# Attention in another written order: projections grouped, six leading key units, weight clamps on GpSimd

## The chip, the cores and the metric

The kernel runs on one core of one Trainium2 chip. The metric is the device time of one execution in microseconds (us), the median of several runs.

## What is computed

```python
def phi(x):
    proj = np.einsum('bhsd,df->bhsf', x, w_phi)
    proj = proj - np.max(np.abs(proj), axis=-1, keepdims=True)
    return np.concatenate([np.exp(proj), np.exp(-proj)], axis=-1)
q_p, k_p = (phi(q), phi(k))
kv = np.einsum('bhsf,bhsd->bhfd', k_p, v)
z = np.sum(k_p, axis=2)
num = np.einsum('bhsf,bhfd->bhsd', q_p, kv)
den = np.einsum('bhsf,bhf->bhs', q_p, z)[..., None] + 1e-06
attn_out = num / den          # 8 batches, 8 heads, 576 tokens, 64 wide; 128 features

x = attn_out, heads side by side          # 4608 x 512
h = x @ w_in                              # 512 x 2048
g = h * np.tanh(softplus(h))
out = g @ w_out                           # 2048 x 512
```

## The kernel before, in words

The program has two stages. The first, some 272 us, is the attention; the second is the feed-forward network, which forms its products from split weights (a rounded part and the rest, each product taken three times) and reads the attention's output back from device memory. Beside the attention, 16 pieces of the feed-forward weights are converted: a piece is loaded as 64-bit words, and GpSimd, VectorE and ScalarE make 32-bit values of them.

The order of every engine's work is written by hand. Each operation is registered with a time, `at(time, function, ...)`; at the end all are sorted by that time and issued in that order. The times set nothing but the order: each engine, and each DMA queue (all transfers here are issued by SP), works through its own instructions in the order written and waits for what it needs.

The attention has 36 units of keys and 36 units of queries (`NU`), each of 512 rows of a pair of heads. The keys run ahead of the queries by `LEAD` units; then a step takes one unit of each.

- A key unit: `k_load` (SP), `k_proj` (TensorE, 16 matmuls into a buffer of the pool `ps_a`, which has two for keys and queries together), `k_center` (VectorE: the largest absolute value, L270, and the subtraction, L271), `k_exp` (ScalarE: two exponentials, L315 and L316), `k_sum` (TensorE, L318, tile names kvps: e times v, accumulated over the rows of a pair of heads). A pair of heads has 4.5 tiles of 128 rows, so every ninth tile is shared by two pairs; a unit with a shared tile has 80 matmuls of sums instead of 64. When a pair's rows are all in, `k_store` (ScalarE, L341) copies its sums out of PSUM. `v_load` (SP) fetches a pair's values into one of three buffers.
- A query unit: `q_load`, `q_proj` (TensorE, pp_q), `q_center` (VectorE), `q_turn` (TensorE, dt: 16 transposes of the centred projection into two PSUM banks), `q_exp` (ScalarE, L371, four exponentials, two for each bank), `q_num` (TensorE, num: the exponentials times the pairs' sums, into two PSUM banks), `q_den` (ScalarE, L391), `q_norm` (VectorE: the reciprocal, L396, and the division, L399), `q_out` (TensorE, xt: four transposes of x), `q_store` (ScalarE, L415, and a DMA to device memory).
- dt, num, xt and the sums share the pool `ps_b` of four PSUM banks.
- TensorE's tile shapes: projections and dt have 64 rows and 128 columns, xt 128 by 128, sums and num 128 rows and 64 columns, the shared tile's sums 64 rows.
- A weight piece: an absolute value on ScalarE (L164), clamp, shift, sign and scale on VectorE (L167, L171, L175, L181), then `low` on GpSimd (L185 and L187), and either a total, four sums, a cast on ScalarE (L215) and a difference, or the cast and two more on GpSimd. The shift reads what the clamp wrote.

The order of one step on TensorE is: quotients of unit n, sums, dt of the next unit, keys' projection, x's transposes, queries' projection. The steps' times are `base(step)` plus constants: `L_AT` for the leading key units, `K_AT` and `Q_AT` for the steps, `T_AT` for the last query units. Weight pieces are due every 14.719 (`CONV`), that is two steps:

```python
at(t + a[0], k_proj, u)
at(t + a[1], k_center, u)
at(t + a[2], k_exp, u)
at(after + a[3], k_sum, u)
at(after + a[4], k_store, u)
...
at(end + a[4], q_num, u)
at(end + a[5], q_den, u)
at(end + a[5] + 0.05, q_norm, u)
at(close_by + a[6], q_out, u)
```

Of the kernel before, what the change touches and what calls it, by code (L numbers as in the profile page):

```python
# [16 lines left out]
P = 128  # L17
# [31 lines left out]
CONV = (13.41, 14.719)  # L49
# [26 lines left out]
def attention_then_mish(ctx, tc, qT, kT, va, w_phi, w_in, w_out, w_out2, out):  # L76
# [71 lines left out]
    def weight_ops(kind, fp, k, quiet):  # L148
# [17 lines left out]
        def clamp():  # L166
            nc.vector.tensor_scalar(w(), w(), LARGE, SMALL, op0=ALU.min, op1=ALU.max)  # L167
# [10 lines left out]
        def scale():  # L178
            t = mid.tile([P, 512], F32, tag="t", name=f"t_{kind}_{fp}_{k}", bufs=1)
            piece[key].append(t)  # L180
# [36 lines left out]
        def lo():  # L217
            dst = piece[key][3]
# [3 lines left out]
        def rest():  # L222
            dst = piece[key][3]
            eng.tensor_sub(w(), w(), dst[:, 0].bitcast(F32))

        def lo_out():
            dst = piece[key][3]
# [3 lines left out]
        def done():  # L231
            staged[key] = piece.pop(key)[3]
# [3 lines left out]
        def spill(h):  # L236
            dst = piece[key][3] if key in piece else staged[key]
# [6 lines left out]
        rest_ops = [(2.2, low)]  # L244
# [20 lines left out]
    def center(parts, name):  # L265
        e = att.tile([P, 2, 2, 512], F32, tag="e", name=f"e_{name}", bufs=5)
        m = att.tile([P, 2, 4], F32, tag="m", name=f"m_{name}", bufs=4)
        to = e[:, :, 0, :].rearrange("p j (n f) -> p j n f", f=F)
        for a, b, ps in parts:
            nc.vector.tensor_reduce(m[:, :, a:b], ps[:, :, a:b], axis=AX.X, op=ALU.max, apply_absolute_value=True)  # L270
# [11 lines left out]
    kv, kv_ps, v_live, k_live = {}, {}, {}, {}  # L282
# [24 lines left out]

    def k_center(n):
        k_live[n] = center(k_live.pop(n), f"k_{n}")

    def k_exp(n):
        e = k_live[n]
        for a, b in zip(cuts_of(n), cuts_of(n)[1:]):
            cols = slice(a * P, b * P)
            nc.scalar.activation(e[:, :, 1, cols], e[:, :, 0, cols], AF.Exp)  # L315
            nc.scalar.activation(e[:, :, 0, cols], e[:, :, 0, cols], AF.Exp, scale=-1.0)  # L316

    def k_sum(n):  # L318
        es = k_live.pop(n)
        tiles = [list(pairs_of(t)) for t in range(4 * n, 4 * n + 4)]  # L320
        for i in sorted(range(4), key=lambda i: len(tiles[i])):
# [6 lines left out]
            for j in range(2):  # L328
                for s in range(2):
                    for r, (p, slot) in enumerate(tiles[i]):  # L330
                        rows = slice(r * D, (r + 1) * D) if shared else slice(0, P)
                        halves(kv_ps[p][:, j, s], es[rows, j, s, i * P:(i + 1) * P], (v_live[p][rows, slot, j, :],) * 2,
                               start=(p in fresh and j == s == 0), stop=(slot == 4))
            for p, slot in tiles[i]:
                if slot == 4:
                    del v_live[p]

    def k_store(n):
# [626 lines left out]
```

## Time and profile before

| | |
|---|---|
| median of 3 runs | 1021.35 us (1021.35, 1023.08, 1020.93) |
| span of the profiled execution | 1021.3 us; its own time beside the span is not given apart from the three runs |
| TensorE busy | 1008.5 us (99%) |
| VectorE, ScalarE, GpSimd busy | 733.3 (72%), 497.7 (49%), 307.1 (30%) us |

In the rows below PE is TensorE's matmuls, PEld its weight loads, DVE VectorE, ACT ScalarE, POOL GpSimd, SP the queue that issues the transfers. L262 is line 262 of the kernel. A timeline's row has the start and the length in us, the engine, the line, the operation, out<-in, the count, and in brackets the idle time before it with what ended it. A matmul's end is modelled; the distance of starts is what two neighbours cost. A row that groups instructions has busy us and the mean of one in ns, then the idle time before them.

### The profile page before, as it was taken

The page shows a single profiled execution, that of the slowest core. Times are in us where ns is not written, and L with a number is a line of the kernel's source. Part 1 is how long each engine was busy: PE and PEld are TensorE (multiplying, and loading weights), DVE is VectorE, ACT ScalarE, POOL GpSimd, SP SyncE. Part 2 cuts the span into 40 slices and gives each one's busy share as a digit, 9 for nine tenths or more (in the row PEclk, how much of TensorE's full clock was granted, in tenths as well). Part 3 has the DMA queues.
Part 4 walks back from the last instruction along what each step waited for, and adds up shares of the span by engine and source line. Part 5 has one row for each costly group of instructions (what it writes and reads, how often), then busy time and mean ns, then how long its engine had stood idle before and what let it go on. Part 6 is the DMA issues. An engine that isn't in the chain of part 4 may idle for free.

```text
span 1021.3 us, 28170 instructions
## 1 busy us (share of the span) xinstructions
PE 1008.5 (99%) x12136; PEld 952.4 (93%) x12136; DVE 733.3 (72%) x1161; ACT 497.7 (49%) x863; POOL 307.1 (30%) x263
## 2 busy tenths in 40 slices
PE   8999999999999999999999999999999999999998
PEld 7889999998889999999999999999999999999998
DVE  6999999988568867658576572466767667667666
ACT  5778777877665434344343433343332333333322
POOL 0454435544513464544746430001101001011011
PEclk9999999999999999999999999999999999999999
DMA  6555567776698676476655768983362451532621
GB/s 208 184 179 184 176 209 256 250 240 200 250 337 311 256 263 219 153 261 243 213 208 172 262 216 313 367 320 105 124 227 65 164 189 60 207 140 88 228 83 42
DMA packets 89292, 208.62 MB, mean 204 GB/s; under 512 B 7376, under 2 KB 35792, under 8 KB 86352
## 3 DMA queue, kind: packets, MB, share of 16 engines
q1 hardware_dynamic: 89168, 206.83, 57.8%
q8 instruction: 95, 1.56, 0.6%
q14 instruction: 29, 0.24, 0.1%
HBM read 122.91 MB, written 83.89 MB: 202 GB/s over the span
## 4 chain that ended last, share of the span: by engine, by line
PE 97%; ACT 1%; DVE 1%; issue 1%; DMA 0%; SPq 0%; DVEq 0%; ACTq 0%
PE h L486 35%; PE o L613 19%; PE o L636 18%; PE num L279 7%; PE kvps L279 7%; PE pp_q L262 4%; PE pp_k L262 3%; PE dt L366 2%; PE xt L408 2%; ACT e_q L371 0%; DMA kraw<-kT 0%; ACT xc L454 0%; DVE m_q L270 0%; DVE x L399 0%; PE z L636 0%
## 5 line engine op out<-in xcount | busy, mean ns | idle before, releaser
L486 PE MATMUL h<-xc,win 128*128 128x256 f32 x3024 | 381.5, 283 | 0.3 <-DVE u L514 0.3
L486 PEld LDWEIGHTS h<-xc,win 128*128 128x128 f32 x3024 | 375.3, 192 | 6.1 <-DVE u L514 0.5
L613 PE MATMUL o<-wout,gh 128*128 128x512 f32 x576 | 144.3, 392 | 0.0
L708 POOL TENSOR_TENSOR part<-part,du 128x512 f32<-128x512 f32 x18 | 23.4, 1298 | 387.9 <-DVE du L698 387.9
L613 PEld LDWEIGHTS o<-wout,gh 128*128 128x128 f32 x576 | 103.6, 189 | 18.7
L518 DVE TENSOR_TENSOR u<-h,u 128x512 f32<-128x512 f32 x72 | 49.6, 688 | 95.2 <-PE h L486 95.1
L636 PE MATMUL o<-wa,gh 128*128 128x256 f32 x576 | 104.4, 282 | 0.0
L636 PEld LDWEIGHTS o<-wa,gh 128*128 128x128 f32 x576 | 88.6, 190 | 0.1
L636 PE MATMUL o<-wa,gl 128*128 128x256 f32 x288 | 80.2, 283 | 0.0
L279 PE MATMUL kvps<-v,e_k 128*64 128x65 f32 (+1 forms) x2560 | 77.2, 222 | 1.6 <-issue 1.6
L636 PE MATMUL o<-wb,held 128*128 128x256 f32 x636 | 77.9, 282 | 0.2 <-DVE du L698 0.2
L636 PEld LDWEIGHTS o<-wb,held 128*128 128x128 f32 x636 | 76.9, 188 | 0.4 <-DVE du L698 0.4
L613 PE MATMUL o<-wout,gl 128*128 128x512 f32 x288 | 77.1, 389 | 0.0
L279 PE MATMUL num<-kv,e_q 128*64 128x65 f32 x2304 | 76.5, 223 | 0.6 <-ACT e_q L371 0.4
L371 ACT ACTIVATE e_q<-dt 128x512 f32<-128x512 f32 x144 | 74.4, 604 | 4.7 <-PE dt L366 4.2
L279 PEld LDWEIGHTS num<-kv,e_q 128*64 128x64 f32 x2304 | 71.2, 137 | 5.4 <-ACT e_q L371 1.2
L279 PEld LDWEIGHTS kvps<-v,e_k 128*64 128x64 f32 (+1 forms) x2560 | 72.5, 137 | 3.7 <-issue 2.1
L506 DVE TENSOR_TENSOR u<-h,p 128x256 f32<-128x256 f32 x72 | 30.1, 418 | 56.2 <-ACT p L493 56.2
L534 ACT ACTIVATE sb<-h 128x256 f32<-128x256 f32 x36 | 13.8, 384 | 105.1 <-PE h L486 71.2
L613 PEld LDWEIGHTS o<-wout,gl 128*128 128x128 f32 x288 | 54.0, 188 | 11.5 <-DVE gl L555 0.4
L493 ACT COPY p<-h 128x256 f32<-128x256 f32 x72 | 26.4, 366 | 69.5 <-PE h L486 69.1
L537 ACT ACTIVATE u<-u 128x768 f32<-128x768 f32 x36 | 30.5, 846 | 56.6 <-DVE u L518 56.6
(99 smaller groups left out, 1662.5 us busy)
## 6 DMA issues: line engine op xcount, KB each, us to landing
xc_spill<-xc SPq DMA_DIRECT2D x63, 512.0 KB, 4.1
xc<-xc_spill SPq DMA_DIRECT2D x63, 512.0 KB, 5.1
x<-x_spill SPq DMA_DIRECT2D x22, 512.0 KB, 6.4
o_part<-part SPq DMA_DIRECT2D x11, 1024.0 KB, 5.0
part<-o_part SPq DMA_DIRECT2D x11, 1024.0 KB, 5.9
in_spill<-wst_in SPq DMA_DIRECT2D x24, 448.0 KB, 2.7
win<-in_spill SPq DMA_DIRECT2D x12, 896.0 KB, 6.8
v<-va SPq DMA_DIRECT2D x32, 325.0 KB, 3.9
```

The costliest lines, as they stand in the source:

```text
L262: nc.tensor.matmul(ps[:, j, n], src, w_phi2[rows], start=True, stop=True)
L279: nc.tensor.matmul(ps[rows], lhsT[:, rows], rhs[h], start=start, stop=stop, skip_group_check=True)
L366: nc.tensor.transpose(turned[n, h][:, jj, i], e[rows, jj, 0, i * P:(i + 1) * P], ident[rows, rows])
L371: nc.scalar.activation(e[:, s, h], ps, AF.Exp, scale=2.0 * s - 1.0)
L486: nc.tensor.matmul(ps, w, x, start=(i in (0, 2) and m == 0), stop=(m == 5), skip_group_check=True)
L493: nc.scalar.copy(p1, h_live[n][0][:, 0])
L506: nc.vector.tensor_tensor(u2, hx[:, 1], u_live[n][0], op=ALU.add)
L518: nc.vector.tensor_tensor(u[:, 0:3:2] if second(n) else u[:, 1:3], hy, u2.unsqueeze(1).broadcast_to([P, 2, CH]), op=ALU.add)
L537: nc.scalar.activation(u[:, 0:3], u[:, 0:3], AF.Mish)
L613: nc.tensor.matmul(o_live[s][tt], g[:, 2 * f + which, cols], wout[fp][:, f, k], start=(first and g is gh and f == k == 0), stop=(last and ...
L636: nc.tensor.matmul(ps, g, w, start=(start and k == 0), stop=(stop and k == 2), skip_group_check=True)
L708: nc.gpsimd.tensor_tensor(cross, cross, d_live[s, tau][0].unsqueeze(1).broadcast_to([P, 2, CH]), op=ALU.add)
```

## The change

The steps' order on TensorE becomes: queries' transposes, queries' projection, keys' projection, the sums of a shared tile, x's transposes of an earlier unit, sums of one or two tiles, quotients, sums of the last two tiles. Six key units lead instead of four. The quotients are formed bank by bank, and each bank gets its own division (a reciprocal each). The largest value and the subtraction of a key unit become two operations of VectorE's order, with the first half of a query unit's division between them; the two exponentials of a key unit are apart in the same way on ScalarE. A pair's sums are stored as soon as all its tiles are in, at either of two places of a step. The weight clamps of the first 16 pieces go to GpSimd, `low` is cut in two (`low`, `scaled`), and a piece's operations get times of their own within four steps.

```diff
--- before.py
+++ after.py
-LEAD = 4
-LEAD_STEP = 3.04
-L_AT = (0.0, 2.62, 3.19, 7.71, 9.38)
-STEP = 7.341
+LEAD = 6
+LEAD_STEP = 3.0
+ENDING = 4
+STEP = 6.95
 TAIL_STEP = 5.73
-LOAD_AT = (-10.994, -0.87, -9.498, -12.558)
-V_AT = (-5.9, -5.9, -5.9, 4.4, 2.0)
+LOAD_AT = (-8.7, 0.3, -10.5, -12.558)
+V_AT = (-5.9, -5.9, -5.9, -2.0, -2.0)
-K_AT = (-1.011, 1.881, 3.585, 3.13, 4.2)
-Q_AT = (1.52, 3.149, 6.11, 6.455, 1.875, 3.0, 6.564, 9.042)
+K_AT = (1.37, 3.9, 5.7, 3.85, 5.0, 2.3, 2.87, 3.1, 5.68, 6.3)
+Q_AT = (0.48, 1.45, 0.0, 0.7, 1.9, 3.81, 4.9, 5.1, 6.1, 0.01, 2.41, 3.2)
 T_AT = (0.95, 2.19, 4.9, 5.3, 8.55, 10.92, 12.6, 13.1)
+BITS_AT = (6.4, 7.0, 14.2, 14.25, 21.15)
+SUMS_AT = (7.1, 21.6, 22.9, 24.2, 24.8, 25.4, 26.0, 27.2, 28.2)
+PLAIN_AT = (7.1, 21.6, 20.3, 23.0, 24.4)
-CONV = (13.41, 14.719)
...
         def clamp():
-            nc.vector.tensor_scalar(w(), w(), LARGE, SMALL, op0=ALU.min, op1=ALU.max)
+            (nc.vector if quiet else nc.gpsimd).tensor_scalar(w(), w(), LARGE, SMALL, op0=ALU.min, op1=ALU.max)
...
             nc.gpsimd.tensor_scalar(f, piece[key][0][:, 0], 2.0 ** -52, None, op0=ALU.mult)
+
+        def scaled():
+            f = piece[key][1][:, 4:8].rearrange("p b m -> p (b m)")
             t = piece[key][2]
             nc.gpsimd.tensor_tensor(t, f, t, op=ALU.mult)
...
-    def center(parts, name):
+    def largest(parts, name):
+        m = att.tile([P, 2, 4], F32, tag="m", name=f"m_{name}", bufs=4)
+        for a, b, ps in parts:
+            nc.vector.tensor_reduce(m[:, :, a:b], ps[:, :, a:b], axis=AX.X, op=ALU.max, apply_absolute_value=True)
+        return parts, m
+
+    def center(parts, m, name):
...
-    def k_exp(n):
+    def k_exp(n, signs=(1, 0)):
         e = k_live[n]
         for a, b in zip(cuts_of(n), cuts_of(n)[1:]):
             cols = slice(a * P, b * P)
-            nc.scalar.activation(e[:, :, 1, cols], e[:, :, 0, cols], AF.Exp)
-            nc.scalar.activation(e[:, :, 0, cols], e[:, :, 0, cols], AF.Exp, scale=-1.0)
+            for s in signs:
+                nc.scalar.activation(e[:, :, s, cols], e[:, :, 0, cols], AF.Exp, scale=2.0 * s - 1.0)
+
+    def k_order(n):
-    def k_sum(n):
-        es = k_live.pop(n)
         tiles = [list(pairs_of(t)) for t in range(4 * n, 4 * n + 4)]
-        for i in sorted(range(4), key=lambda i: len(tiles[i])):
+        order = sorted(range(4), key=lambda i: -len(tiles[i]))
+        shared = [i for i in order if len(tiles[i]) == 2]
+        rest = order[len(shared):]
+        return shared, rest[:2 - len(shared)], rest[2 - len(shared):]
+
+    def k_sum(n, part):
...
+        for i in k_order(n)[part]:
...
-    def k_store(n):
-        for p in [p for p in sorted(kv_ps) if (p + 1) * S <= (n + 1) * 512]:
+    def k_store():
+        for p in [p for p in sorted(kv_ps) if left[p] == 0]:
...
-        for j in range(2):
-            for i in range(2):
+        for i in range(2):
+            for j in range(2):
                 for t in range(2):
...
+    def q_norm(n, i):
+        x, r = x_live[n], r_live[n]
+        nc.vector.reciprocal(r[:, i], r[:, i])
+        nc.vector.tensor_tensor(x[:, i].rearrange("p t (j d) -> p t j d", d=D), num_live.pop((n, i))[:, :, :, :D],
+                                r[:, i].unsqueeze(3).broadcast_to([P, 2, 2, D]), op=ALU.mult)
...
-        return min(step, NU - LEAD) * STEP + max(0, step - NU + LEAD) * TAIL_STEP
+        return min(step, NU - ENDING) * STEP + max(0, step - NU + ENDING) * TAIL_STEP
...
+        t, at_exp, at_sum = base(u - LEAD), base(u - LEAD + 1), base(u - LEAD + 2)
+        a = K_AT
         if u < LEAD:
...
+            at(t - 11.1, k_load, u)
+            at(t + V_AT[min(u, 4)], v_load, u)
+            at(t, k_proj, u)
+            at(t + 0.5, k_first, u)
+            at(t + 1.0, k_exp, u)
+        else:
+            at(t + LOAD_AT[0], k_load, u)
+            at(t + LOAD_AT[1], v_load, u)
+            at(t + a[0], k_proj, u)
+            at(t + a[1], k_largest, u)
+            at(t + a[2], k_center, u)
+            at(at_exp + a[3], k_exp, u, (1,))
+            at(at_exp + a[4], k_exp, u, (0,))
+        if u < LEAD - 2:
+            at(at_sum + (-0.1 if u == 0 else 1.2), k_sum, u, 0)
+            at(at_sum + (-0.1 if u == 0 else 1.2), k_sum, u, 1)
+            at(at_sum + 1.3, k_sum, u, 2)
+            at(at_sum + 2.0, k_store)
+        else:
+            at(at_sum + a[5], k_sum, u, 0)
+            at(at_sum + a[6], k_sum, u, 1)
+            at(at_sum + a[7], k_store)
+            at(at_sum + a[8], k_sum, u, 2)
+            at(at_sum + a[9], k_store)
...
+        at(t + a[0], q_proj, u)
+        at(t + a[1], q_center, u)
+        at(after + a[2], q_turn, u)
+        at(after + a[3], q_exp, u, 0)
+        at(after + a[4], q_exp, u, 1)
+        at(after + a[5], q_num, u)
+        at(after + a[6], q_den, u, 0)
+        at(after + a[7], q_norm, u, 0)
+        at(after + a[8], q_den, u, 1)
+        at(max(end + a[9], after + a[8] + 0.1), q_norm, u, 1)
+        at(end + a[10], q_out, u)
+        at(end + a[11], q_store, u)
...
+        if i < 4 * HALF:
+            t = base(2 * i)
+            at(t - 8.0, weight_load, *pc)
+            for delay, (_, op) in zip(BITS_AT, bits):
+                at(t + delay, op)
+            times = SUMS_AT if len(sums) == len(SUMS_AT) else PLAIN_AT
```

## Rows read from the trace of the kernel before

**Rows 1.** The page: busy us, share of the span, instructions.
```profile
PE 1008.5 (99%) x12136; PEld 952.4 (93%) x12136; DVE 733.3 (72%) x1161; ACT 497.7 (49%) x863; POOL 307.1 (30%) x263
```

**Rows 2.** The chain of waits, first 300 us, shares by line.
```profile
by line: PE num L279 23.7%; PE kvps L279 22.4%; PE pp_q L262 12.0%; PE pp_k L262 11.5%; PE dt L366 6.6%; PE xt L408 6.2%; PE h L486 5.2%; PE o L613 2.9%; issue 2.1%; ACT e_q L371 1.6%; DMA kraw<-kT 1.4%; ACT xc L454 0.9%; DVE m_q L270 0.8%;
```

**Rows 3.** Stages, us: PE, PEld, DVE, ACT, POOL busy, clock, DMA, GB/s.
```profile
176.96:184.27 7.31, 7.31 (x199) 6.76 (x200) 6.92 (x9) 5.39 (x11) 5.99 (x7) 1.00 0.61 218
...
sum 36.11, PE 36.11 PEld 33.57 DVE 34.10 ACT 28.34 POOL 21.75; mean PE 7.22 PEld 6.71 DVE 6.82 ACT 5.67 POOL 4.35
```

**Rows 4.** Timeline of PE, one step without a shared tile.
```profile
184.20 2.11 PE L279 MATMUL num<-kv,e_q 128*64 128x65 f32 x64
186.12 2.06 PE L279 MATMUL kvps<-v,e_k 128*64 128x65 f32 x64
188.11 0.71 PE L366 MATMUL dt<-ident,e_q 64*128 64x64 f32 x16
188.66 1.11 PE L262 MATMUL pp_k<-head,kraw 64*128 64x128 f32 x16
189.70 0.66 PE L408 MATMUL xt<-ident,x 128*128 128x128 f32 x4
190.28 1.16 PE L262 MATMUL pp_q<-head,qraw 64*128 64x128 f32 x16
191.37 2.08 PE L279 MATMUL num<-kv,e_q 128*64 128x65 f32 x64
```

**Rows 5.** Timeline of PE, a query projection right behind a key projection.
```profile
22.22 1.16 PE L262 MATMUL pp_k<-head,kraw 64*128 64x128 f32 x16
23.22 1.06 PE L262 MATMUL pp_q<-head,qraw 64*128 64x128 f32 x16
```

**Rows 6.** Timeline of PE, xt followed by a matmul of its shape.
```profile
279.68 0.60 PE L408 MATMUL xt<-ident,x 128*128 128x128 f32 x4
280.03 3.84 PE L486 MATMUL h<-xc,win 128*128 128x256 f32 x30
```

**Rows 7.** Timeline, first 45 us: two waits of PE, and one releaser.
```profile
27.95 1.22 DVE L271 TENSOR_TENSOR e_q<-pp_q,m_q 128x1024 f32<-128x1024 f32 x1
...
29.27 1.16 PE L262 MATMUL pp_q<-head,qraw 64*128 64x128 f32 x16 [1.39 <-issue]
...
44.24 1.16 PE L262 MATMUL pp_q<-head,qraw 64*128 64x128 f32 x16 [0.31 <-DVE e_q L271]
```

**Rows 8.** Lines, first 280 us (the last row: durations min/median/max in ns).
```profile
L396 DVE RECIPROCAL r<-r 128x8 f32<-128x8 f32 x36 | 7.3, 202 | 15.3 <-ACT r L391 14.5
L167 DVE TENSOR_SCALAR w_in<-w_in 128x512 f32<-128x512 f32 x8 | 3.9, 489 | 0.0
L185 POOL TENSOR_SCALAR w_in<-words_in 128x512 f32<-128x512 uint32 x8 | 12.4, 1552 | 19.1 <-DMA words_in<-w_in 18.5
...
L171 DVE TENSOR_SCALAR w_in<-w_in x8: 426/838/845, 26.4 to 185.6; 128x512 uint32<-128x512 uint32 x8
```

**Rows 9.** ScalarE: timeline of a step, and the cast's line.
```profile
184.16 0.71 ACT L164 ACTIVATE w_in<-words_in 128x512 f32<-128x512 f32 x1
...
188.46 0.36 ACT L341 COPY kv<-kvps 128x260 f32<-128x260 f32 x1
188.89 2.06 ACT L371 ACTIVATE e_q<-dt 128x512 f32<-128x512 f32 x4
...
L215 ACT CAST wst_in<-w_in 128x896 fp32r<-128x896 f32 x4 | 3.8, 940 | 0.1
```

**Rows 10.** Timeline of PE, the attention's ending.
```profile
246.11 0.71 PE L366 MATMUL dt<-ident,e_q 64*128 64x64 f32 x16
...
254.69 0.66 PE L408 MATMUL xt<-ident,x 128*128 128x128 f32 x4 [0.68 <-ACT e_q L371]
...
261.60 0.63 PE L408 MATMUL xt<-ident,x 128*128 128x128 f32 x4 [0.48 <-DVE x L399]
...
271.27 0.71 PE L366 MATMUL dt<-ident,e_q 64*128 64x64 f32 x16
```

More of the change, by code (lines that the diff above doesn't have):

```diff
@@ L179, in scale @@
             t = mid.tile([P, 512], F32, tag="t", name=f"t_{kind}_{fp}_{k}", bufs=1)
-            piece[key].append(t)
+            piece[key].insert(2, t)
             nc.vector.tensor_scalar(t.bitcast(U32), w().bitcast(U32), 0xFF800000, None, op0=ALU.bitwise_and)
@@ L217, in lo @@
         def lo():
-            dst = piece[key][3]
+            dst = piece[key][-1]
             eng.tensor_sub(dst[:, 1], piece[key][1][:, 1:8], dst[:, 0].bitcast(F32))
@@ L222, in rest @@
         def rest():
-            dst = piece[key][3]
+            dst = piece[key][-1]
             eng.tensor_sub(w(), w(), dst[:, 0].bitcast(F32))
         def lo_out():
-            dst = piece[key][3]
+            dst = piece[key][-1]
             eng.tensor_tensor(dst[:, 1], w(), piece[key][2], op=ALU.add)
@@ L231, in done @@
         def done():
-            staged[key] = piece.pop(key)[3]
+            staged[key] = piece.pop(key)[-1]
             if fp < 2:
@@ L236, in spill @@
         def spill(h):
-            dst = piece[key][3] if key in piece else staged[key]
+            dst = piece[key][-1] if key in piece else staged[key]
             where = in_spill[fp, k] if kind == "in" else out_spill[fp, k] if fp < HALF else out_spill2[fp][:, :, :, k]
@@ L243, in weight_ops @@
         ops = [(0.0, absolute), (0.9, clamp), (1.35, shift), (1.8, sign), (2.5, scale)]
-        rest_ops = [(2.2, low)]
+        rest_ops = [(1.2, low), (1.0, scaled)]
         if blocks:
@@ L760, in attention_then_mish @@
-        if u >= NU - LEAD:
-            after = end = close_by = t
-        a = T_AT if u >= NU - LEAD else Q_AT
-        early = 0.49 if u == 1 else 0.0
-        at(t + LOAD_AT[2] - early, q_load, u)
-        at(t + a[0] - early, q_proj, u)
-        at(t + a[1] - early, q_center, u)
-        for j in range(2):
-            at(after + a[2] + 0.45 * j - early, q_turn, u, j)
-            at(after + a[3] + 1.2 * j - early, q_exp, u, j)
-        at(end + a[4], q_num, u)
-        at(end + a[5], q_den, u)
@@ new lines, in attention_then_mish @@
+        if u < LEAD - 2:
[9 more added lines that the diff above has]
+            at(at_sum + a[9], k_store)
+        t, after, end, a = base(u), base(u + 1), base(u + 2), Q_AT
@@ new lines, in attention_then_mish @@
+        at(t + LOAD_AT[2], q_load, u)
+        if u >= NU - ENDING:
+            a = T_AT
+            at(t + a[0], q_proj, u)
+            at(t + a[1], q_center, u)
+            at(t + a[2], q_turn, u)
+            at(t + a[3], q_exp, u, 0)
+            at(t + a[3] + 1.2, q_exp, u, 1)
+            at(t + a[4], q_num, u)
+            for i in range(2):
+                at(t + a[5], q_den, u, i)
+                at(t + a[5] + 0.05, q_norm, u, i)
+            at(t + a[6], q_out, u)
+            at(t + a[7], q_store, u)
+            continue
@@ L821, in attention_then_mish @@
             at(clock, op)
-            if pc[1] >= 2 and j in (high, len(sums) - 1):
+            if j in (high, len(sums) - 1):
                 at(clock + SPILL_AT[j > high], spill, int(j > high))
```

84 lines of the change are left out of this document (38 added, 46 removed).

## The prediction

> **What bounds the kernel now.** I read the page first: TensorE is busy 99% of the span [rows 1]. The change touches only the attention, which ends at about 272 us; the feed-forward part behind it, some 750 us, issues the same instructions. So I went to the chain of waits of the first 300 us: it runs through TensorE's own instructions, with 2.1% "issue" and no other engine above 1.6% [rows 2]. Then the busy time by stages: five steps in the middle of the attention last 36.11 us, in which TensorE is busy 36.11, VectorE 34.10, ScalarE 28.34 and GpSimd 21.75, and the granted clock is 1.00, the 2.4 GHz level [rows 3]. A step (one unit of queries, one of keys) thus takes 7.22 us and is bound by TensorE's order, with VectorE only 0.40 us behind. Nothing but TensorE's order can gain there; VectorE can soon lose.
>
> Inside a step the starts of TensorE's groups give what each costs, its change of tile shape included [rows 4]: num 1.92, the keys' sums (kvps) 1.99, the queries' transposes (dt) 0.55, the keys' projection (pp_k) 1.04, x's transposes (xt) 0.58, the queries' projection (pp_q) 1.09; together 7.17. A step whose sums hold a tile shared by two pairs takes 7.31 [rows 3].
>
> **The middle: one change of shape less.** The new order is dt, pp_q, pp_k, (shared sums), xt, half of the sums, num, the other half. Now pp_q stands behind xt; then both projections stand behind dt, which has their tile shape. Where a query projection already follows a key projection, their starts lie 1.00 apart [rows 5]. At most 1.04 + 1.09 - 2 x 1.00 = 0.13 goes; at least the 0.05 by which the projection behind xt exceeds the one behind dt. I take 0.11, near the first, since its row shows the new neighbours themselves. xt's own end stays: followed by another 128x128 matmul xt takes 0.35 [rows 6], by another shape 0.58, and the sums behind it are another shape again. From the second dt to the 31st there are 29 steps: 29 x 0.11 = **3.2 us gained** (1.5 to 3.8).
>
> **The start.** Four key units led; now six do. Work is moved, not removed, so only TensorE's idle time counts: 1.39 us where the third query projection waits for its PSUM buffer, that is for VectorE's subtraction of the second (27.95 + 1.22 = 29.17, projection at 29.27), and later 0.31 for the same reason [rows 7]. In the new order key projections stand there. A leading unit asks VectorE for 2 x 1.22 us and TensorE for 1.0 + 2.0, so VectorE catches up 0.5 per unit, and by my walk through the order the eighth key projection finds its buffer 0.2 late. **1.5 gained** (0, if the wait only moves, to 1.7). On SP's queue the fourth value load now stands ahead of the first query load, the seventh key load and the first weight load, and waits for the first pair's buffer, as it did before; between that release and its use lie the rest of unit 1's sums, a projection and unit 2's sums, some 4.5 us. I cost it at nothing; without that cover it costs 1 to 2 us once, as a bound. The weight loads are issued 14 us ahead of their use: nothing.
>
> **VectorE and GpSimd.** A weight piece (every second step) loses a clamp of 0.49 and each query unit gains a second reciprocal of 0.20 [rows 8]: per two steps 2 x 6.82 - 0.49 + 0.40 = 13.55, against 7.17 + 7.31 - 2 x 0.11 = 14.26 of TensorE. It fits, with 0.7 to spare. GpSimd's clamp isn't in the trace; it lies between VectorE's 0.49 and the 1.55 of GpSimd's own tensor-scalar of that size [rows 8], and I take the latter, the same engine. GpSimd is busy 60% of the middle and the shift that waits for the clamp is written 7.2 us behind it: hidden. Behind the clamp on GpSimd's queue stand `low` and `scaled`, whose results are needed 14 us later. Without that cover a late shift would hold up the next query unit's centring behind it on VectorE.
>
> On the port the two engines share, the row first: VectorE's shift takes 0.43 at the shortest, 0.84 in the median, where it runs beside GpSimd, and never over 0.85 [rows 8]. The Trainium skill ("SBUF — State Buffer", "SBUF: two separate sides") says that the shared port pair is an exclusive lock and the loser blocks for the other's whole instruction; the row does not agree with a whole 1.55. By the row, more work on GpSimd costs VectorE at most 0.42 per operation, which the 0.7 holds. By the page's rule the sum would be that of the fourth rival.
>
> **ScalarE, in order.** A query unit's four exponentials start 0.78 after dt and take 2.06 [rows 4, 9]: done 2.84 after dt. Now num comes 3.26 after dt; then 0.55 + 1.00 + 1.04 + 0.58 + 0.98 = 4.15, so there is more room. But in every second step a cast (up to 0.94) and an absolute value (0.71) are written ahead of the exponentials, and the store of finished sums (0.36) ahead of both waits for the sums' end [rows 9]. Where these meet, the exponentials end at 4.2 to 4.4, up to 0.25 late; at worst in every fourth step: 29 / 4 x 0.25 = 1.8. I take **1.0 lost** (0 to 1.8), about half, since a late step starts the next with room.
>
> **The four PSUM banks** hold sums, dt, xt and num. Now num stands before the sums, and both its banks have been read when the next dt comes. Then the second half of num is normalised only behind the next dt, and dt needs two of the other three banks. Where a pair's sums close with the step's last matmul while the next pair is already open, dt waits for the store: 0.36 [rows 9] and a hand-over of 0.10 [rows 7] on either side, 0.6. Eight pairs close in nine steps: one like this, two more half a sum earlier, 0.1 each, the rest in time. 29 / 9 x 0.8 = 2.6. ScalarE's lateness hides behind some of it: **0.9 lost** (0 to 2.6).
>
> **The ending.** From the 31st dt to the 36th now 25.16 us pass, with waits of 0.68 and 0.48 at xt [rows 10]. The old order issues the 32nd and 33rd dt together, and their num together. The new one alternates dt, pp_q, xt, num: num stands 2.17 behind dt and its exponentials 2.84, 0.7 late (unit 31). At unit 32 a normalising copy and the last weight cast stand between the two halves of the exponentials: xt 1.2 and num 0.4 late. At unit 30 cast and absolute value stand ahead of the exponentials: 0.9. That is 3.2, less the 0.68 and 0.48 that stood there: 2.0. I take **1.6 lost** (0 to 2.3).
>
> **Sum.** -3.2 - 1.5 + 1.0 + 0.9 + 1.6 = -1.2. The profile gives no time of its execution beside the span of 1021.3, 0.05 below the median of 1021.35 (runs 1020.93 to 1023.08). From the median: **1020.2 us** (rounded up). All terms at their good ends give -5.5, 1015.8; all at their bad ends +5.2, 1026.6. A measurement of this kernel tells some 0.2% (2.0 us) from no change: the forecast is "same".
>
> **Rivals.** First, *the waits don't come*: ScalarE is idle 1.55 us of each step [rows 3], and stores and late casts could slip into that, and the ending's waits into each other. Then -3.2 - 1.5 + 0.5 = -4.2: 1017.1, faster. Against it: ScalarE works in written order, so idle time ahead of a waiting store helps nothing behind it.
>
> Second, on the other side, *dt waits for its banks*. The place is TensorE's first transpose of a step, the price 0.6 where the store comes last; it decides once all three closings of nine steps pay it: 1.8 x 29 / 9 = 5.8. With the ending at 2.3: 1021.35 - 4.7 + 5.8 + 2.3 = 1024.8, slower. Against it: now dt finds its banks at once [rows 4], and two of the three closings come half a sum earlier.
>
> Third, *the change of shape isn't what pp_q pays for*, and the order doesn't do what it is written for: the step stays, and -1.5 + 3.5 = +2.0 gives 1023.4, at the edge of slower. Against it: the 1.00 of [rows 5].
>
> Fourth, *GpSimd blocks VectorE*: shift and sign wait once and the scale once for a whole GpSimd instruction of 1.55: 13.55 + 3.1 = 16.65 per two steps, 2.4 over TensorE, x 14.5 = 35 us slower, 1055. The shift's longest in these pieces, 0.85, is against it. It is what the port rule cited above would make of this kernel.
>
> **How the numbers follow.** Forecast 0.38 (same); first rival 0.37 (faster); second 0.20, third 0.03, fourth 0.02 (slower, together 0.25). The range leaves out the fourth and the meeting of all bad ends, and reaches to the other rivals with the spread of their terms: 1015.6 to 1025.4. The forecast alone: 1018.8 to 1022.6.
>
> **What would show it.** Right: steps of 7.05 to 7.10 without a shared tile; pp_q and pp_k 1.00 apart; no wait near 1.4 at a projection in the first 60 us; short waits of num on exponentials in every second step and of dt on the store of sums; xt and num of units 31 and 32 late. Wrong: steps of 7.17 and TensorE never idle (third); dt waiting in most steps (second); a shift or scale over 0.9 (fourth); a middle without any wait (first). A step under 6.95 would show that I misread what a change of shape costs.

## The result, and the profile after

The changed kernel takes 1034.77 us (median of 4 runs, 1034.1 to 1034.98), against 1021.59 of the kernel before on the same chip: ratio 1.0125, 95% interval [1.0111, 1.0139]. It is 13 us slower. The prediction (1020.2, at most 1025.4) missed it. In all later executions the time is at least 1.7 us above the span, mostly 1.8. So the trace before, with a span of 1021.3, is most likely that of the slowest of its three runs (1023.08) and not one at the median, as the prediction took it. The two traces therefore show 11.9 us of the 13.2.

Where the time lies is seen by cutting both traces at four places: the start of the second dt, of the 31st and of the 36th, and the first product of the feed-forward's output (o). First the stretches of the kernel before, then of the one after; a row has the stretch, its length, the busy time of TensorE's matmuls and weight loads, VectorE, ScalarE and GpSimd, then the granted clock, the DMA share and GB/s.

```profile
0.00:34.41 34.41, 28.27 (x673) 26.43 (x674) 25.23 (x28) 20.23 (x28) 6.03 (x12) 1.00 0.67 209
34.41:246.11 211.70, 210.56 (x5434) 195.45 (x5429) 193.24 (x261) 167.42 (x318) 97.40 (x88) 1.00 0.64 209
246.11:271.27 25.16, 23.35 (x554) 20.87 (x549) 16.42 (x25) 19.25 (x45) 16.92 (x14) 1.00 0.59 209
271.27:285.68 14.41, 14.15 (x174) 13.57 (x172) 5.16 (x13) 7.89 (x16) 5.68 (x5) 1.00 0.83 274
```

```profile
0.00:35.79 35.79, 29.35 (x672) 27.10 (x673) 24.56 (x24) 20.67 (x29) 2.84 (x8) 1.00 0.59 186
35.79:249.45 213.66, 206.75 (x5415) 193.88 (x5412) 188.90 (x277) 163.51 (x315) 107.03 (x102) 1.00 0.64 204
249.45:276.79 27.34, 25.22 (x570) 22.23 (x566) 19.88 (x33) 19.88 (x46) 18.92 (x16) 1.00 0.45 159
276.79:297.53 20.74, 15.88 (x175) 15.37 (x174) 5.13 (x14) 8.53 (x17) 9.50 (x8) 0.84 0.86 298
```

I call them lead, middle, ending and join (the hand-over from the attention to the feed-forward). They grew by 1.38, 1.96, 2.18 and 6.33 us, 11.85 of the 11.9 between the spans (1033.2 and 1021.3); what follows lasts 735.7 against 735.6. One key projection (about 1.0) has moved from the middle into the lead, and one query projection from the lead into the ending; like for like the middle lost 3.0 and the ending 1.1. The largest loss, the join, has no term in the prediction.

A step of the new order where nothing waits, in the timeline of TensorE after:

```profile
139.68 0.71 PE L398 MATMUL dt<-ident,e_q 64*128 64x64 f32 x16
140.23 1.11 PE L267 MATMUL pp_q<-head,qraw 64*128 64x128 f32 x16
141.18 1.06 PE L267 MATMUL pp_k<-head,kraw 64*128 64x128 f32 x16
142.16 0.66 PE L437 MATMUL xt<-ident,x 128*128 128x128 f32 x4
142.75 1.15 PE L288 MATMUL kvps<-v,e_k 128*64 128x65 f32 x32
143.73 2.04 PE L288 MATMUL num<-kv,e_q 128*64 128x65 f32 x64
145.60 1.10 PE L288 MATMUL kvps<-v,e_k 128*64 128x65 f32 x32
146.63 0.59 PE L398 MATMUL dt<-ident,e_q 64*128 64x64 f32 x12
```

It takes 6.95 us against 7.17 of [rows 4]; with a shared tile 7.11 against 7.31 of [rows 3]. The two projections cost 0.95 + 0.98 instead of 1.04 + 1.09. So 29 steps give 29 x 0.2 = 5.8 us, and a middle that is 3.0 longer hides waits of 8.8. The waits of TensorE from 30 to 300 us (total us, times, longest) follow; the kernel before has 0.8, 0.7, 0.5 and 0.3 in the same view up to 262 us. "Issue" is a wait that no semaphore explains; what it is, the last section shows.

```profile
PE h L515 <- DVE u L535: 4.9, 1, 4.9
PE dt L398 <- DVE x L428: 2.9, 4, 0.8
PE num L288 <- ACT e_q L403: 2.5, 7, 1.1
PE num L288 <- issue: 1.9, 1, 1.9
PE kvps L288 <- issue: 1.0, 1, 1.0
PE dt L398 <- ACT wout L220: 0.8, 1, 0.8
PE xt L437 <- DVE x L428: 0.7, 1, 0.7
PE xt L437 <- ACT e_q L403: 0.7, 1, 0.7
```

**The bank.** In the dt of units 1, 2, 3 and 12 the first transpose starts and the second waits 0.77 us. In the timeline after:

```profile
35.79 0.27 PE L398 MATMUL dt<-ident,e_q 64*128 64x64 f32 x1
...
36.26 0.42 DVE L428 TENSOR_TENSOR x<-num,r 128x256 f32<-128x256 f32 x1
...
36.83 0.68 PE L398 MATMUL dt<-ident,e_q 64*128 64x64 f32 x15 [0.77 <-DVE x L428]
```

The division of num's second half ends 0.15 before dt goes on. In the built program dt's second half sits in num's second bank for just these units, and for 21 and 30. Such a dt adds 1.0 to its step.

**The long step**, 219.00 to 228.92, 9.9 us instead of 7.1:

```profile
212.92 2.10 POOL L224 TENSOR_TENSOR wst_in<-w_in,wst_in 128x896 fp32r<-128x896 f32 x1 [1.05 <-ACT wst_in L220]
213.11 2.46 DVE L177 SCALAR_TENSOR_TENSOR w_out<-words_out,w_out 128x512 uint32<-128x512 uint32 x1
...
216.31 0.33 SPq L312 DMA_DIRECT2D v<-va  x1
216.73 2.79 SPq L244 DMA_DIRECT2D in_spill<-wst_in  x2
...
222.89 0.62 ACT L220 CAST wst_out<-w_out 128x512 fp32r<-128x512 f32 x1 [3.60 <-DMA in_spill<-wst_in]
```

The sign takes 2.46 us instead of 0.69 beside GpSimd's `lo` (L224, the rest that a weight's rounded part leaves). The division behind it is late, and dt waits 0.59 for it. On SP's queue a value load stands until 216.31, with both spills (stores to device memory) of the weight piece behind it; the next piece's cast waits 3.60 for the single staging buffer, the exponentials behind it on ScalarE, and num for those (1.07 and less).

**The join**, as a chain from GpSimd to TensorE:

```profile
263.75 1.28 POOL L192 TENSOR_TENSOR t_out<-w_out,t_out 128x512 f32<-128x512 f32 x1 [6.30 <-DVE t_out L183]
264.99 1.27 POOL L474 TENSOR_TENSOR xs<-x 128x512 f32<-128x512 f32 x1
...
272.62 1.28 POOL L484 TENSOR_TENSOR xc<-x,xc 128x512 fp32r<-128x512 f32 x1
...
283.69 9.39 SPq L445 DMA_DIRECT2D x_spill<-xs  x3
...
292.15 0.59 ACT L444 COPY xs<-xt 128x512 f32<-128x512 f32 x1 [8.92 <-DMA x_spill<-xs]
...
293.04 0.42 DVE L535 TENSOR_TENSOR u<-h,p 128x256 f32<-128x256 f32 x1 [6.96 <-ACT p L522]
...
293.52 4.21 PE L515 MATMUL h<-xc,win 128*128 128x256 f32 x18 [4.86 <-DVE u L535]
```

The last early weight piece waits on GpSimd for VectorE's scale, which is written behind a query unit of the ending. The feed-forward's x sums (L474) and x blocks (L484, the rests of x's rounded parts) stand behind it on that queue, the blocks' spills on SP's, there the store of xs behind them, on ScalarE the copy that needs its buffer and the p copy, then VectorE and TensorE. The 4.21 for 18 matmuls is a fallen clock (below).

### The profile page after: what moved, and what is told of

It reads as the page before. It is cut to its first block, busy times and chain, and to the rows that moved or that the text cites. A ratio compares the mean times of both kernels' runs of the same rounds, so it can differ in the third digit from the quotient of the medians.

```text
span 1033.2 us, 28245 instructions
## 1 busy us (share of the span) xinstructions
PE 1009.3 (98%) x12136; PEld 954.5 (92%) x12136; DVE 732.6 (71%) x1181; ACT 494.7 (48%) x863; POOL 319.7 (31%) x279
## 4 chain that ended last, share of the span: by engine, by line
PE 91%; POOL 2%; issue 2%; DMA 1%; DVE 1%; ACT 1%; SPq 1%; DVEq 0%; ACTq 0%; POOLq 0%
PE h L515 34%; PE o L642 19%; PE o L665 17%; PE kvps L288 6%; PE num L288 4%; PE pp_k L267 3%; PE pp_q L267 3%; PE dt L398 2%; PE xt L437 2%; DMA x_spill<-xs 1%; POOL xc L484 1%; DVE e_k L280 0%; ACT e_q L403 0%; POOL xs L474 0%; DVE x L428 0%
## 5 line engine op out<-in xcount | busy, mean ns | idle before, releaser
L288 PE MATMUL kvps<-v,e_k 128*64 128x65 f32 (+1 forms) x2560 | 86.5, 225 | 1.0 <-issue 1.0
L288 PEld LDWEIGHTS kvps<-v,e_k 128*64 128x64 f32 (+1 forms) x2560 | 76.1, 138 | 9.3 <-issue 5.9
L339 ACT ACTIVATE e_k<-e_k 128x1024 f32<-128x1024 f32 (+1 forms) x74 | 76.8, 1038 | 9.2 <-DVE e_k L330 9.0
```

The costliest lines, as they stand in the source:

```text
L288: nc.tensor.matmul(ps[rows], lhsT[:, rows], rhs[h], start=start, stop=stop, skip_group_check=True)
L339: nc.scalar.activation(e[:, :, s, cols], e[:, :, 0, cols], AF.Exp, scale=2.0 * s - 1.0)
```

## The experiments

Lead, middle, ending and join, worked out from the starts in each timeline, the span of that execution, the median, and the ratio to the kernel before on the same chip:

| kernel | lead | middle | ending | join | span | median | ratio, 95% |
|---|---|---|---|---|---|---|---|
| before | 34.41 | 211.70 | 25.16 | 14.41 | 1021.3 | 1021.59 | |
| after | 35.79 | 213.66 | 27.34 | 20.74 | 1033.2 | 1034.77 | 1.0125 |
| e1 | 33.07 | 218.62 | 32.43 | 14.41 | 1034.1 | 1034.10 | 1.0123 [1.0108, 1.0138] |
| e2 | 33.94 | 217.38 | 27.30 | 19.66 | 1033.9 | 1034.45 | 1.0112 [1.0090, 1.0134] |
| e3 | 33.67 | 223.02 | 27.33 | 20.80 | 1040.4 | 1040.83 | 1.0186 [1.0171, 1.0201] |
| e5 | 33.02 | 219.88 | 27.33 | 19.96 | 1035.8 | 1038.28 | 1.0165 [1.0141, 1.0188] |
| e7 | 33.22 | 216.62 | 27.32 | 19.98 | 1032.8 | 1033.42 | 1.0113 [1.0096, 1.0130] |
| e8 | 33.49 | 217.74 | 27.52 | 15.29 | 1029.4 | 1029.97 | 1.0083 [1.0068, 1.0098] |
| e9 | 33.92 | 216.24 | 27.53 | 14.98 | 1028.1 | 1027.91 | 1.0060 [1.0040, 1.0079] |
| e10 | 32.95 | 216.67 | 27.33 | 20.78 | 1034.1 | 1035.13 | 1.0130 [1.0115, 1.0145] |
| e11 | 33.25 | 212.35 | 27.62 | 14.51 | 1023.2 | 1024.74 | 1.0027 [1.0015, 1.0039] |
| e12 | 33.70 | 210.57 | 25.16 | 14.40 | 1019.4 | 1021.80 | 0.9998 [0.9988, 1.0007] |
| e13 | 34.16 | 213.43 | 27.89 | 16.93 | 1027.8 | 1025.54 | 1.0032 [1.0019, 1.0045] |
| e14 | 34.13 | 207.12 | 27.68 | 15.04 | 1019.4 | 1022.29 | 1.0009 [0.9998, 1.0021] |
| e15 | 35.04 | 207.16 | 26.47 | 16.28 | 1020.3 | 1023.08 | 1.0006 [0.9996, 1.0015] |
| e16 | 34.05 | 207.84 | 26.47 | 16.08 | 1019.8 | 1022.52 | 1.0002 [0.9992, 1.0011] |

**e1, the last weight piece earlier.**

```diff
-for delay, (_, op) in zip(BITS_AT, bits):
+for delay, (_, op) in zip(BITS_AT[:4] + (14.3,) if i == 15 else BITS_AT, bits):
...
+if i == 15:
+    times = (7.1, 15.0, 16.0, 17.0, 18.0)
```

> Only the last of the 16 early weight pieces is moved: its scale, scaled, hi, rest and lo_out are written some 7 to 10 us earlier, ahead of the x sums instead of around them; every other instruction keeps its order. Theory (the feed-forward's join is lost on GpSimd's queue, where the last piece's 'scaled' waits 6.30 us for VectorE's scale with the x sums behind it): the stretch from the last dt to the first output product falls from 20.7 us to 14.4 to 15.5, the p copy on ScalarE no longer waits 8.9 us behind the xs copy, and the whole comes to 1028 to 1029.5 us. Rival (the join is late because TensorE's clock falls there or because the attention itself ends late): the stretch stays at 19 to 21 us and the time within 1.5 us of 1034.8. Rival (the shared port: x sums beside VectorE): the waiting moves but less than 3 us return, 1032 to 1034.

The join is 14.41, as forecast, the time is not: the ending grew by 5.1. The piece's cast, now early, waited for the staging buffer, with the next exponentials and a dt (3.37 us) behind it:

```profile
265.73 0.62 ACT L220 CAST wst_out<-w_out 128x512 fp32r<-128x512 f32 x1 [4.78 <-DMA out_spill<-wst_out]
```

The edit gave back the join and made a second case of the long step.

**e2, the second division ahead of the keys' subtraction.**

```diff
-at(after + a[8], q_den, u, 1)
-at(max(end + a[9], after + a[8] + 0.1), q_norm, u, 1)
+at(after + 4.95, q_den, u, 1)
+at(after + 5.65, q_norm, u, 1)
```

> Only the second half's denominator and division are moved: they are written ahead of the key unit's subtraction on VectorE instead of behind it. Theory (dt waits for the bank that the second half of num holds until its division): the waits of 0.77 us at dt of units 1, 2, 3 and 12 and of 0.26 at unit 30 go, since the bank is free some 1.2 us earlier; 3 to 4 us return, 1031 to 1032. Rival (dt waits for the store of a finished pair's sums, as the prediction had it): the same dt still wait 0.7 to 0.8 us and the time stays within 1 us of 1034.8. Rival (the earlier division makes VectorE wait for num and so holds up the keys' subtraction behind it): pp_q or pp_k wait in most steps, steps of 7.0 turn to 7.2 or more, and the time rises to 1037 to 1040.

The waits at units 1, 2, 3 and 12 are gone (steps of 7.16, 7.32, 7.16): the bank was released by the division, not by the store. But no time came back. In three later steps pp_k starts 0.21 late, behind the subtraction that now comes late. Two steps of 8.3 and 8.6 stand at a sign of 2.47, with stalls called "issue" of 0.68 and 0.78 in them. The long step took 11.4; behind its wait of 1.49 the clock fell to 0.50.

**e3, the clamps back on VectorE.**

```diff
-(nc.vector if quiet else nc.gpsimd).tensor_scalar(w(), w(), LARGE, SMALL, op0=ALU.min, op1=ALU.max)
+nc.vector.tensor_scalar(w(), w(), LARGE, SMALL, op0=ALU.min, op1=ALU.max)
```

> Only the clamps of the first 16 weight pieces go back from GpSimd to VectorE; the order is that of after. Theory (the clamps have next to no share in the loss): 1033.5 to 1036, the join of 20.7 us and the waits of dt stay, VectorE is busier by 16 x 0.49 = 7.8 us. Rival (the clamp on GpSimd fills its queue, delays the last piece and blocks VectorE's SBUF instructions): the join shrinks by 3 us or more and no sign instruction takes over 0.9 us, 1027 to 1031. Rival (VectorE is the bound and needed the relief): steps with a weight piece lengthen by up to 0.5, 1038 to 1041.

6 us slower, the last rival's figure: dt waits 9.2 us in all on divisions (2.9 after). With the clamp ahead of it, the shift now stands beside `lo` in five pieces (1.9 to 2.3 us instead of 0.42), and one sign took 2.46. So moving the clamps is worth 6 us in the new order, and they did not make the join late. How much of it is the clamps' own 7.8 us on VectorE and how much the long shifts isn't shown.

**e5, shift and sign behind the query unit's subtraction.**

```diff
-BITS_AT = (6.4, 7.0, 14.2, 14.25, 21.15)
+BITS_AT = (6.4, 7.0, 15.5, 15.55, 21.15)
```

> Only the shift and sign of each of the first 16 weight pieces are moved on VectorE: from ahead of the query unit's maximum to behind its subtraction, 1.3 us later as written and 2.4 us later in time, so that they don't start while GpSimd's 2.1 us 'lo' of the piece before runs. Theory (one sign of 2.46 us beside 'lo' set off a chain of late VectorE work that cost the step at 219 us 2.8 us): no sign over 0.85 us, the longest step of the middle falls from 9.9 to 7.2 us, 2.5 to 3.5 us return, 1031 to 1032.5. Rival (the long step comes from the DMA of the weight piece that the cast waited 3.60 us for, and the sign only shares its moment): the sign is short, the step still takes over 9 us, 1034 to 1035. Rival (signs stay long wherever they stand): signs over 2 us appear at other places, time within 1.5 us of 1034.8.

No sign over 0.7 outside the ending, yet the long step stayed at 9.5 and num waited 1.45 there: the spill makes that step. 3.5 us were lost: the divisions behind the sign came later and dt waited 1.50 for two of them, and behind the first the clock fell to 0.50.

**e7, the value loads behind the spills on SP's queue.**

```diff
-LOAD_AT = (-8.7, 0.3, -10.5, -12.558)
+LOAD_AT = (-8.7, 3.05, -10.5, -12.558)
```

> Only the written time of the value loads in the middle is moved on SP's queue, from 0.3 to 3.05 us of the step: each stands behind the spill of a weight piece's two halves instead of ahead of it. Every compute engine's order is unchanged. Theory (the long step at 219 us comes from SP's queue: a value load waited there for its buffer, both spills of the last 'in' piece stood behind it, the cast into the single staging buffer waited 3.6 us for them, and with it ScalarE's exponentials and num): the cast's wait falls below 1 us, that step from 9.9 (11.2 to 12.8 in the other kernels) to 7.0 to 7.5 us, and 2.5 to 4 us return: 1030.5 to 1032.5. Rival (the DMA engines are full there, whatever the order: share 0.97 to 0.99): the spills start earlier but land late, the step keeps 9 us or more, and the time stays within 1 us of 1034.8.

```profile
213.13 2.50 SPq L244 DMA_DIRECT2D in_spill<-wst_in  x2
216.64 0.33 SPq L312 DMA_DIRECT2D v<-va  x1
```

The spills go 3.6 us earlier, the cast finds its buffer at once (219.52), num's wait there is gone. The step is 8.2, from 9.5 to 12.8 in the others, with a dt wait of 0.96 left. So the cast's wait was the queue's, not that of full DMA engines; what is left of the step waits for VectorE. Of the median 1.4 to 1.7 came back, less than forecast.

**e8, only the scale of the last piece earlier** (the first line of e1's diff).

> Only VectorE's scale of the last early weight piece is written 6.85 us earlier, right behind that piece's sign; nothing else moves. Theory (GpSimd's 'scaled' of that piece waits 6.30 us for it, with the x sums, the x blocks, their spills, the xs copy and the p copy behind): GpSimd's x sums start some 5 to 6 us earlier, the stretch from the last dt to the first output product falls from 20.7 to 14.4 to 15.5 us as in the kernel whose last piece was moved whole, but the ending stays at 27.3 us since the cast stays where it was: 1028 to 1029.5 us. Rival (what was gained there is lost again ahead of it, as in that kernel): the ending grows by the same amount, 1033 to 1035.

Join 15.29, ending 27.5, 1029.97: GpSimd's `scaled` waits 1.16 instead of 6.30, the x sums start at 262.08 instead of 264.99 though the ending began 1.8 later, the h products wait 0.35 instead of 4.86. The join's cause is settled.

**e9, the edits of e2, e7 and e8 together.**

> The second division ahead of the keys' subtraction, the value loads behind the spills and the early scale of the last piece, together. Theory (three separate losses that add: bank waits 3 to 4 us, the long step 3 to 4, the join 6.3): 1034.8 - 3 - 3 - 6.3 = 1022 to 1024 us, so the changed order about level with the kernel before; what is left over the 5.9 us that 29 shorter steps give is TensorE's short stalls that no semaphore explains. Rival (what one wait gives back turns up in another, as with the second division alone, which left the time where it was): 1026 to 1029.

1027.9, the rival's figure: the join's 6 us came back, of the other two little. Two signs of 2.46 us stand at 80 and 96 us, each beside `lo`; the dt behind them wait 0.54 and 0.37. The steps of 8.6 and 8.3 there hold stalls called "issue" of 0.35 and 0.94, and this trace has the most of these, 4.8 us in all.

**e10, the changed kernel again.**

> The changed kernel once more, unchanged. Theory (the dt waits of units 1, 2, 3, 12 and 30, the long step at 219 us and the join of 20.7 us are in the written order; the stalls shown as 'issue' are chance): all of these return within 0.3 us, the long step between 9.5 and 12 us, while the 'issue' stalls of 1.88 us at 33.5 us and 0.96 us at 182.4 us fall elsewhere; the second dt then starts near 33 to 34 us instead of 35.8. Rival (the 'issue' stalls are fixed by the program too): they stand at the same two places. Time 1034 to 1036.

Bank waits, long step (9.46) and join (20.78) return; the stalls called "issue" fall at other places, and the lead is 32.95 where the first trace, with a stall of 1.88 in it, has 35.79. That is 1.46 under the lead before, but the trace before has a stall of 0.79 in its own lead, at 21.33. The same TensorE order without it (e12) has 33.70, so the new lead gained 0.75. The wait at a projection didn't go; it fell from 1.39 (1.00 in e12) to 0.67, in the trace after 0.66:

```profile
28.51 1.16 PE L267 MATMUL pp_k<-head,kraw 64*128 64x128 f32 x16 [0.66 <-PE pp_q L267]
```

**e11, as e9 with the sign beside the scale.**

```diff
-BITS_AT = (6.4, 7.0, 14.2, 14.25, 21.15)
+BITS_AT = (6.4, 7.0, 14.2, 21.1, 21.15)
```

> The kernel of the three edits together, and VectorE's sign of each early weight piece written one step later, right ahead of its scale (21.1 instead of 14.25), so that it falls in the step without GpSimd's 2.1 us 'lo'. Theory (a two-input instruction of VectorE that starts while GpSimd's 'lo' runs is held until that ends, 2.46 instead of 0.69 us, and the keys' and the divisions behind it come late): no sign over 1.1 us outside the ending, the steps of 8.3 to 8.6 us near 86 to 103 us fall to 7.0 to 7.6, and the time from 1027.9 to 1024.5 to 1026.5. Rival (in the new place it meets GpSimd's clamp and 'low' of the next piece and is held there): signs of 1.2 us and more, 1027 to 1030. Rival (the long signs are a sign and not a cause: late steps bring them about): signs short, time within 1 us of 1027.9.

1024.74: 3.2 us less, the middle 3.9 shorter, no sign over 1.10 before the ending. But the stalls called "issue" fell from 4.8 us in e9's trace to 0.9, and that alone is 3.9; less these stalls both middles are 211.4. In the four steps from the first long sign on, stalls taken off, e9 is 0.9 longer. So a long sign does make the dt behind it late, and two of them cost about 1 us; the rest of the 3.2 isn't shown to be theirs.

**e12, the clamps alone on GpSimd, in the kernel before.**

> The kernel before with one part of the change alone: the clamps of its early weight pieces on GpSimd. Theory (in the old order VectorE is 0.40 us per step behind TensorE and no wait shows, so relief buys nothing, and GpSimd has room): 1020.5 to 1022.5, no new wait of TensorE over 0.3 us. Rival (the relief is worth the 5 to 6 us that taking it back costs in the new order): 1016 to 1018. Rival (more work on GpSimd holds VectorE): signs or shifts over 0.9 us, 1023 to 1026.

No change: 1021.80. A clamp takes GpSimd 0.61 us. The old order's waits for VectorE behind the lead, 0.31 at a projection and 0.48 at xt, stay as they were.

**e13, as e9 without shift and sign.**

> The kernel of the three edits together, with the shift and the sign of the 16 early weight pieces left out, so that those weights keep clamped magnitudes; VectorE has 1.1 us less in every second step and no instruction beside 'lo' but the scale. Theory (VectorE in its written order, 0.4 us per two steps short of the new TensorE order, is what holds the new steps back): the stretch from the second to the 31st dt falls from 216.2 to 207 to 211 us, dt waits on divisions vanish, 1019 to 1023. Rival (TensorE's stalls without a visible cause, and ScalarE): the stretch stays at 213 us or more, 1025 to 1028.

The middle is 213.43, the rival's figure, but stalls called "issue" of 2.66 are in it, and behind the longest, 2.04, the clock fell to 0.50: the next step took 8.68 against 7.11 in e9. Without both it would be about 209, an estimate. So this run doesn't decide. Waits of dt on divisions are gone, as the theory had it. With 1.1 us less per two steps on VectorE, pp_k still follows pp_q by 1.16 instead of 0.95 in steps such as the one at 55.81. The join grew by 2.0: h waits 1.99 there.

**e14, as e11, with the early division only where dt needs the bank.**

```diff
+early = u in (0, 1, 2, 11, 20, 29)
+at(after + (4.95 if early else a[8]), q_den, u, 1)
+at(after + 5.65 if early else max(end + a[9], after + a[8] + 0.1), q_norm, u, 1)
```

> As the kernel with the sign beside the scale, but the second division stands ahead of the keys' subtraction for units 0, 1, 2, 11, 20 and 29 alone, whose bank the next dt's second half takes; in all other units it stands behind it, as in the changed kernel. Theory (the earlier division removes dt's bank waits in those units, and in every other unit only makes the keys' subtraction late, for which pp_k waits 0.22 us): pp_k again follows pp_q by 0.95 us in most steps, the stretch from the second to the 31st dt falls from 212.4 to 207 to 210 us, and the time from 1024.7 to 1020 to 1022.5, level with the kernel before or a little under it. Rival (the 0.22 us at pp_k only makes up for lateness that then shows at xt, num or dt): the stretch stays at 211.5 us or more, 1023.5 to 1025.5. Rival (the banks are dealt out differently once divisions move, and other dt wait): dt waits of 0.7 us at new units, 1026 or more.

```profile
34.13:241.25 207.12, 205.91 (x5416) 193.54 (x5412) 189.58 (x275) 163.21 (x316) 108.85 (x102) 1.00 0.66 211
```

The middle falls by 5.2 to 207.12, TensorE busy in 205.91 of it: the order's gain appears, with all of VectorE's work in place. Of the 5.2, 0.9 are stalls called "issue" that this trace doesn't have. pp_k follows pp_q by 0.95 in every step, where e11 has eight steps with 1.16. The profiled execution took 1021.14, 1.1 under the median of 1022.29; the medians fell by 2.4 from e11, which makes it level with the kernel before.

**e15 and e16, the ending.** In the last three units both halves of the exponentials ahead of the casts; e16 also writes the cast of the first 'out' piece 3.7 us later.

```diff
-at(t + a[3] + 1.2, q_exp, u, 1)
+at(t + a[3] + (0.05 if u > NU - ENDING else 1.0), q_exp, u, 1)
```

> The kernel that divides first only where needed, and in the last three units ScalarE runs the two halves of a unit's exponentials one behind the other, with the feed-forward's casts behind them (for the fourth from the end only the weight cast moves behind). Theory (num of the last units waits 0.42 + 0.15 us for exponentials behind casts): these waits go, the ending falls from 27.7 to 26.3 to 26.9 us, 1020.8 to 1021.8 us. Rival (the casts are then late, and GpSimd's x blocks behind them): the join grows from 15.0 to 15.8 or more and the time stays at 1022 to 1023.

> As e15, and the cast of the first 'out' piece (and the two operations behind it) written 3.7 us later, behind a unit's exponentials, so that it no longer stands ahead of them while the staging buffer is still being written out. Theory: the cast's wait of 1.53 us is gone or hides nothing, the steps of 7.83 and 7.60 us at 212 and 220 us fall to 7.0 to 7.2, 0.8 to 1.3 us under e15. Rival (other late work takes its place there): the two steps together stay above 15 us and the time is that of e15 within 0.5.

The ending falls by 1.2, and the join grows by 1.2: the xs copy waits 5.42 instead of 4.18 us for the stores of xs, and the h products 1.36 behind it. No cast is late there, so the rival had the figure and not the reason: the end of the attention now waits for those transfers. e16 takes the step at 214 us to 7.0 and the next is 7.9. Both are level with the kernel before; none of these versions beats it by what can be told.

## Why the prediction was wrong

- **What follows the attention** is the step that failed most. The prediction took the feed-forward as untouched because it "issues the same instructions", and costed `low` and `scaled` as needed 14 us later. For the last piece the work behind them is the x sums. This cost 6.33 us; e8 and e1, which move that piece's scale, give it back.
- **"The four PSUM banks"**, 0.9 (up to 2.6): dt waits, but for the second division in num's bank, not for the store. It cost four dt 1.0 each; e2 shows the releaser, e14 that the wait can go without a price. The second rival had the place and not the cause.
- **SP's queue**, costed at nothing: I looked at who needs the value load, not at what stands behind it. The spills do, and the cast behind them. That step took 2.3 to 2.8 us more than 7.12 in the two traces of the kernel; e7 takes 1.3 to 1.8 of it back, and the rest is VectorE's lateness.
- **"VectorE and GpSimd ... It fits, with 0.7 to spare"**: as a sum it does (e14 has all of it in steps of 6.95). In order it did not: a late VectorE shows at dt or pp_k.
- **The fourth rival, at 0.02**: its figure of 35 us is far off, its mechanism acts. The shift's 0.85 stood beside `low`; the new order puts the sign beside `lo`. The two long signs of e9 cost about 1 us against e11. The price that the rival set, each shift and sign of a piece held for a whole GpSimd instruction, never came.
- **The change of shape** was right in kind and too small: 0.20 a step instead of 0.11, 5.8 us instead of 3.2. The 1.00 of [rows 5] is not the floor: behind dt, projections follow at 0.95.
- **ScalarE, in order**, 1.0 lost: outside the long step, TensorE's waits for exponentials in the middle are one of 0.68 in the first trace and none in e10. The term was too large.
- **The start**, -1.5: the -1.46 of e10 against the trace before agrees by luck. Without the stall of 0.79 in that trace it is -0.75, since a projection still waits 0.67, not 0.2.
- **The ending**, +1.6: near in figure (+1.1), not in the waits. Those over 0.1 us add up to 2.1 against 1.7 before. The longest is xt at 263.39, 0.70 for a division; for exponentials num waits 0.39 and 0.42, at 269.10 and 274.40, where the forecast had 0.9 and 1.2 for units 30 and 32. What the rest of the 1.1 is, isn't shown.
- **The clamp**: 0.61, not 1.55, and hidden; that the move would matter to VectorE I denied, and in the new order it is worth 6 us (e3), in the old nothing (e12).

The stalls called "issue" belong to no term of the prediction: outside the 1.39 of [rows 7], the traces hold 1.6 us of them before, 2.8 after, 3.6 in e10, 4.8 in e9, none in e12 and e14 (those over 0.25 us). Two pairs of traces of one TensorE order, before and e12, after and e10, differ by 1.1 and 3.0 in the middle, and by 0.8 and 2.65 in the stalls there. Less the stalls, the middles are 210.9 before, 212.7 after, 213.1 in e10, 211.4 in e9 and e11 and 207.1 in e14. So middles are to be compared less their stalls.

## What to carry to other kernels

A hand-written order has its cost in what stands behind each instruction on its queue: follow the last instance of every repeated chain to the work that comes after it, and every DMA queue as well. With a bound engine 0.2 us a step faster, engines that were 0.4 us behind become part of the bound; a summed load that fits says nothing about order. Give an early release only to the instances that need it: with the division in front everywhere, pp_k came 0.2 us late in eight steps of e11. And before a difference between two traces is put down to an edit, take off the stalls that come and go between executions of one kernel.

## What the runs showed of the hardware

A VectorE instruction on two SBUF inputs that starts while a two-input GpSimd instruction runs ends after it: the sign took 2.46 us beside a `lo` of 2.10, 1.65 in the ending. In e3 the shift, one input, did too: 2.21 us, begun 0.16 after `lo`. Beside GpSimd's one-input `low` the shift took up to 0.85 [rows 8] and the sign 1.02 (the last row below; `low` ran from 83.23 to 84.82). Reductions and subtractions that read PSUM kept 1.22 beside `lo` (169.79 and 171.05 us of the trace after).

```profile
81.06 2.09 POOL L224 TENSOR_TENSOR win<-w_in,win 128x896 fp32r<-128x896 f32 x1 [1.05 <-ACT win L220]
...
81.22 2.21 DVE L173 TENSOR_SCALAR w_in<-w_in 128x512 uint32<-128x512 uint32 x1
83.47 1.02 DVE L177 SCALAR_TENSOR_TENSOR w_in<-words_in,w_in 128x512 uint32<-128x512 uint32 x1
```

The Trainium skill ("SBUF — State Buffer", "SBUF: two separate sides") calls the shared port pair an exclusive lock: a GpSimd instruction and one of VectorE in a two-port mode or with two SBUF inputs block each other, the later one for the other's whole instruction. Beside `lo` the traces agree; beside `low` they don't, and the measurement decides.

The clock can fall after a wait of TensorE, and that adds to the wait's price. Behind the 4.86 us of the join the granted clock was 0.55, and 18 h products took 4.21 us against 2.41 at 282.94. After the long step of e1 (num had waited 1.70) it was 0.50, the 1.2 GHz level, for three microseconds. The wait's length alone doesn't tell: behind a wait of 1.49 in e2 the clock fell too, while behind the 1.88 at 33.54 of the trace after, and behind its 1.07, it stayed at 1.00.

```profile
294.00:298.00 4.00, 4.00 (x20) 3.94 (x20) 0.66 (x2) 3.26 (x6) 0.13 (x1) 0.55 0.95 309
```

```profile
228.00:231.00 3.00, 3.00 (x60) 3.00 (x56) 2.14 (x5) 1.71 (x4) 2.92 (x3) 0.50 0.88 271
```

The stalls called "issue" are waits for instructions. The 16 traces hold 48 of them over 0.25 us. One is the projection at 29.27 of [rows 7], which started when VectorE's subtraction had ended. The other 47 all stand at the same place: counting TensorE's instructions in order of start, at the 194th or 195th of a group of 256. Each ends 1.17 to 1.58 us after a transfer of 16 KB of instructions has landed, the only kind on queue q8. The trace after has 96 such transfers for TensorE's 24,520 instructions, so one for every 256. The page of the trace after, and two of the stalls:

```profile
q8 instruction: 96, 1.57, 0.6%
```

```profile
33.54 1.32 PE L288 MATMUL num<-kv,e_q 128*64 128x65 f32 x38 [1.88 <-issue]
...
182.36 1.04 PE L288 MATMUL kvps<-v,e_k 128*64 128x65 f32 x28 [0.96 <-issue]
```

The transfers behind these two landed at 32.28 and 181.12. Why such a transfer comes late in one execution and in time in another isn't shown.
